# A new order of the attention stages of pairs 4 to 15, in a linear-attention and mixture-of-experts kernel

## The chip, the cores and the metric

The kernel runs on one core of a Trainium2 chip. A core has five engines with a queue each: TensorE (PE in the profile; PEld is its weight load), VectorE (DVE), ScalarE (ACT), GpSimd (POOL) and SyncE (SP), which here issues nearly all transfers. Each engine takes its instructions in the order of the program and stops at one whose inputs or buffers are not ready. The metric is the device time of one execution in microseconds.

## The reference

Two layers follow each other, in float32. The first is linear attention with batch 4, 8 heads, 576 tokens and head dimension 64; the second a mixture of 4 experts on the 2304 tokens.

```
phi(x):  p = x @ w_phi;  p = p - max|p| over the 128 features
         return concat(exp(p), exp(-p))                # 256 features
q_p, k_p = phi(q), phi(k)
kv  = sum over tokens of k_p^T v        z = sum over tokens of k_p
num = q_p @ kv      den = q_p . z + 1e-6      attn = num / den
x = attn as [2304, 512];  p = domain_probs / (row sum + 1e-9)
out = sum over e of  p[:, e] * (relu(x @ w1[e]) @ w2[e])     # 512 -> 1024 -> 512
```

## The kernel before

**Work.** Attention goes by pairs: one pair is two heads of one batch entry, 16 in all (four batch entries of four pairs). The second layer goes by units: a unit is two blocks of 128 hidden features of one expert, 16 units for each block of tokens. `first_units` runs all 16 units on the first 512 tokens while the attention of pairs 5 to 15 still runs; `second_units` then takes the other tokens in a form with fewer products (seven instead of eight, with sums of blocks, `x_ops` and `s_sums`).

**Float32 out of rounded parts.** Most matmuls take a number as a rounded part (hi) and a rest (lo), and form three products. So each operand needs a rounding copy (`split_pair`, `exps`, `w_hi`) and a subtraction (`lo_part`, `w_lo`).

**The stages of a pair.** `load_pair` fetches keys, queries and values. `split_pair` makes hi and lo. Keys: `proj` (three groups of token tiles), `proj_sub` (maximum and subtraction on VectorE, which frees the bank), `k_exp` on ScalarE, `k_kv` on TensorE; `kv_hi` and `kv_lo` split the result. Queries of pairs 4 to 15 are stacked: hi and lo of one head lie in the two halves of the partitions, so `q_proj` gets the transposed projection at once. There the maximum runs across partitions: `q_max` copies the projection to `dq` on ScalarE and reduces on VectorE, `q_maxT` transposes the partial maxima on TensorE, `q_maxrow` reduces again and writes them to memory (`max_d`), `q_maxin` reads them back into all partitions (`mb`), `q_sub` subtracts them, `q_exp2` takes both exponentials and rounds, `lo_part` makes the rest. Then `q_num` (score products), `q_copy`, and for the denominators a way through memory: `den_out`, `den_in`, `den_recip`, `rec_out`, `rec_in`; `x_mul` is the product of the two, `x_out` and `x_store` pass it on. The queries and the scores have three parts: (0, 0) for the first 256 tokens of both heads, (1, 0) and (1, 1) for the other 320 of each.

**What sets the order.** The schedule is written by hand. Each stage has a key, an offset within the pair plus 16 for each pair, and `later` puts it into a heap. The units give the pace: after each step of three 512-wide matmuls `tick` moves the clock by `clock.step` keys and `run_until` emits all stages whose key has come. So the keys fix the order of each engine's queue, not times. `LAST` (the last `x_out`) sets `clock.step`; after `LAST_IN` (the last use of the attention's input buffers) `to_early` reuses their space, loads tokens for the second stage, and its sums `xa_ops` follow at one key each; `to_late` does the same for the rest.

**Buffers that matter here.** Three PSUM banks `ps_att` serve ten users in a pair of the stacked kind: three key projections, three query projections, the transposed maxima, three score products. The second layer's matmuls (`l2_tile`, L668) have two banks, freed by `out` on VectorE (L678). The exponentials have two buffers `e` (freed by `lo_part`, L330) and five buffers `ehi`, which the keys' exponentials share. Low parts run on VectorE for part (0, 0) and on GpSimd for the two others (`LO_ENG`).

Of the kernel before, what the change touches and what calls it, by code (L numbers as in the profile page):

```python
# [20 lines left out]
def kernel(  # L21
# [16 lines left out]
    nc = tc.nc  # L38
# [9 lines left out]
    NPAIR = B * NP  # L48
# [5 lines left out]
    PER = 16  # L54
# [36 lines left out]
    max_d = dram.tile([NPAIR, 2 * S], F32, name="max_d")  # L91
# [13 lines left out]
    def later(key, fn):  # L105
        heapq.heappush(queue, (key, next(count), fn))

    def run_until(key):
        while queue and queue[0][0] <= key:
            heapq.heappop(queue)[2]()  # L110
# [22 lines left out]
    pairs = [Pair() for _ in range(NPAIR)]  # L133
# [113 lines left out]
    def q_maxrow(i):  # L247
        s = pairs[i]
        s.mrow = ap_.tile([S // 16, 32], F32, name="mrow", tag="mrow", bufs=1)
        nc.vector.tensor_reduce(  # L250
            s.mrow, s.mT[0 : S // 16, 0:P].rearrange("p (a c) -> p c a", c=32), axis=AX.X, op=ALU.max
        )
        nc.sync.dma_start(max_d[i].rearrange("(r c) -> r c", c=32), s.mrow)

    def q_maxin(i):
        s = pairs[i]
# [68 lines left out]
    def lo_part(i, parts, op):  # L325
        engine = {"v": nc.vector, "g": nc.gpsimd}[(LO_ENG0 if i < NP else LO_ENG)[op]]
        if len(parts) > 1:
            e, sl = parts[1]
            lo = ap_.tile([P, 1024], F32R, name="elo", tag="elo", bufs=4)
            engine.tensor_tensor(lo[sl], e[sl], parts[0][sl].bitcast(F32), op=ALU.subtract)  # L330
            parts[1] = lo

    def k_exp(i, c):
        s = pairs[i]
        t4, t4z = (slice(0, 64), slice(64, P)) if s.stack else (slice(64, P), slice(0, 64))
        rows, g = (slice(0, P), 4) if c < 2 else (t4, 2)
        d = s.d["k", c][rows, : g * NF]
        s.ke[c] = exps(d.rearrange("p (g f) -> p g f", f=NF), rows, g, NF, False)
        if c == 2:

            nc.gpsimd.memset(s.ke[c][0][t4z, : 2 * g * NF], 0.0)
# [159 lines left out]
    def x_store(i):  # L501
# [4 lines left out]
        if a < t0 + S:  # L506
            nc.sync.dma_start(xd[hp, :, a : t0 + S], pairs[i].xt[:, a - t0 :])

    STAGES = (
        (-25.6, load_pair, ("kq",)),  # L510
        (-16, load_pair, ("v",)),
        (-7.5, split_pair, ("k",)),
        (-1.9, split_pair, ("q",)),
        (-0.3, proj, ("k", 0)), (0.6, proj_sub, ("k", 0)), (2.7, k_exp, (0,)),
        (7.2, k_kv, (0,)),
        (2.1, proj, ("k", 1)), (2.1, proj_sub, ("k", 1)), (3.9, k_exp, (1,)),
        (10, k_kv, (1,)),
        (2.8, proj, ("k", 2)), (3.4, proj_sub, ("k", 2)), (8.3, k_exp, (2,)),
        (12.2, k_kv, (2,)), (13, kv_hi, ()), (13.2, kv_lo, ()),
    )  # L520
    TAIL = (
        (18.6, q_num, (0, 0)), (19.9, q_copy, (0, 0)),
        (21.5, q_num, (1, 0)), (22, q_copy, (1, 0)),
        (22.7, q_num, (1, 1)), (23.3, q_copy, (1, 1)),
        (26.2, den_out, ()), (29.8, den_in, ()), (31.2, den_recip, ()), (32.5, rec_out, ()),
        (34.7, rec_in, ()), (36.9, x_mul, ()), (40.5, x_store, ()), (37, x_out, ()),
    )
    Q_STAGES = (
        (5.5, proj, ("q", 0)), (6.4, proj_sub, ("q", 0)), (8.4, q_tr, (0, 0)), (9.4, q_exp, (0, 0)),
        (13.7, lambda i: lo_part(i, pairs[i].qe[0, 0], 0), ()),  # L530
        (7.5, proj, ("q", 1)), (10.4, proj_sub, ("q", 1)),
        (14.5, q_tr, (1, 0)), (15.2, q_exp, (1, 0)),
        (16, lambda i: lo_part(i, pairs[i].qe[1, 0], 1), ()),
        (14.5, q_tr, (1, 1)), (15.5, q_exp, (1, 1)),
        (16, lambda i: lo_part(i, pairs[i].qe[1, 1], 2), ()),
    )
    STACK_STAGES = (
        (4.4, q_proj, (0, 0)), (5.2, q_max, (0, 0)),
        (5, q_proj, (1, 0)), (5.8, q_max, (1, 0)),
        (6.6, q_proj, (1, 1)), (7.3, q_max, (1, 1)),  # L540
        (8.6, q_maxT, ()), (9, q_maxrow, ()), (10, q_maxin, ()),
        (13.5, q_sub, (0, 0)), (13.7, q_exp2, (0, 0)),
        (13.9, q_sub, (1, 0)), (14.3, q_exp2, (1, 0)),
        (14.7, lambda i: lo_part(i, pairs[i].qe[0, 0], 0), ()),
        (14.5, q_sub, (1, 1)), (15, q_exp2, (1, 1)),
        (15.4, lambda i: lo_part(i, pairs[i].qe[1, 0], 1), ()),
        (15.8, lambda i: lo_part(i, pairs[i].qe[1, 1], 2), ()),
    )
    SHIFT = 3.5
    for i in range(NPAIR):  # L550
        stack = pairs[i].stack
        for o, fn, args in STAGES + (STACK_STAGES if stack else Q_STAGES):
            later(PER * i + o, functools.partial(fn, i, *args))
        for o, fn, args in TAIL:
            later(PER * i + o + (SHIFT if stack else 0), functools.partial(fn, i, *args))
    FIRST = PER * (NP - 1) + 37
    LAST = PER * (NPAIR - 1) + 37 + SHIFT
    LAST_PS = PER * (NPAIR - 1) + 24 + SHIFT
    LAST_IN = PER * (NPAIR - 1) + 16.1

# [80 lines left out]
    def convert(kind, n, wait):  # L644
# [3 lines left out]
        if kind == "w1" and n >= NU:  # L648
            for o, fn in ((wait[0], s_sums), (wait[0] + 0.5, s_hi), (wait[1], s_lo)):
                later(max(clock.key, LAST + XA_LATE + 1) + o * clock.step, functools.partial(fn, n))  # L650
        else:
# [3 lines left out]
    def l2_tile(n, h, j, tile, o):  # L655

        e = (n % NU) * 2 // NFC
        if n >= NU and tile % 3 == 0:
            ps = ps_kv.tile([P, DM], F32, name="l2", tag="kv")
        elif n < NU and clock.key > LAST_PS:  # L660

# [136 lines left out]
    def spread(ops, start, gap):  # L798
        for i, fn in enumerate(ops):
            after(start + gap * i, fn)  # L800
# [132 lines left out]
    with tc.manual_schedule():  # L933
        nc.vector.memset(wbd, 0.0)
        nc.sync.dma_start(wbd[0:D, 0:NF], w_phi)
        nc.scalar.dma_start(wbd[D:P, NF : 2 * NF], w_phi)
        nc.vector.memset(out0[:, 0, 0:256], 0.0)
        warm = ps_l2.tile([P, 512], F32, name="warm", tag="l2")
        for _ in range(4):
            nc.tensor.matmul(  # L940
                warm[:, 0:256], lhsT=out0[:, 0, 0:P], rhs=out0[:, 0, 0:256], start=True, stop=True
            )
        run_until(STAGES[0][0])
        make_identity(nc, ident)
        nc.vector.memset(eps, 0.0)
        nc.vector.memset(eps[64:P, 0:1], 1e-6)
        nc.vector.memset(eps[0:64, 1:2], 1e-6)
        nc.vector.tensor_copy(wbd_hi, wbd)
        nc.vector.tensor_tensor(wbd_lo, wbd, wbd_hi.bitcast(F32), op=ALU.subtract)
        later(2.1, lambda: nc.sync.dma_start(pr, probs.rearrange("(t p) e -> p t e", p=P)))  # L950

        def probs_norm():
            nc.vector.reduce_sum(prs, pr, axis=AX.X)
            nc.vector.tensor_scalar_add(prs, prs, 1e-9)
            nc.vector.reciprocal(prs, prs)
            nc.vector.tensor_tensor(
                pr, pr, prs.unsqueeze(2).to_broadcast([P, NTT, NE]), op=ALU.mult
            )

        later(20.1, probs_norm)  # L960
        later(30.1, stacked_weights)
        for n in range(2):
            for i, kind in enumerate(("w1", "w2")):
                for o, fn in ((0, w_load), (4, w_hi), (6, w_lo)):
                    later(FETCH[2 * n + i] + o, functools.partial(fn, kind, n))
        run_until(FIRST)
        xa, xb = Pair(), Pair()
        xa.first, xa.nt = N0, 512
        xb.first, xb.nt = N0 + 8, 384
        for x, hi, lo in ((xa, x1_hi, x1_lo), (xb, x0_hi, x0_lo)):  # L970
            x.op = {
                "B11": (hi[:, 0:2, : x.nt], lo[:, 0:2, : x.nt]),
                "B21": (hi[:, 2:4, : x.nt], lo[:, 2:4, : x.nt]),
            }
        out1 = []

        xa_ops = {}

        def to_early():

            in_stack.close()
            early.append(
                ctx.enter_context(
                    tc.tile_pool(name="early", bufs=1, side="right", reuse_waits="tile")
                )
            )
            x_load(xa, xa.first + 4, xa.nt)
            xa_ops.update(x_ops(xa))
            fns = [fn for k in ("t", "T2", "T1", "t3", "T3") for fn in xa_ops[k]]
            for i, fn in enumerate(fns):  # L990
                later(LAST_IN + X_IN + X_GAP * i, fn)

        def to_late():

            att_stack.close()
            late.append(ctx.enter_context(tc.tile_pool(name="late", bufs=1, reuse_waits="tile")))
            out1.append(late[0].tile([P, 4, DM], F32, name="out1"))

        later(LAST_IN, to_early)
        later(LAST + XA_LATE, to_late)  # L1000
        clock.key = FIRST
        clock.step = (LAST - FIRST) / (NU * (2 * NP + 2 * N0) * SPREAD)
        pend = first_units()
        clock.key = max(clock.key, LAST + XA_LATE)
        run_until(clock.key)
        clock.step = 1
        spread([fn for k in ("B22", "t4", "T4") for fn in xa_ops[k]], XA_START, XA_GAP)
        second_units(pend)
# [38 lines left out]
```

## Time and profile before

| | |
|---|---|
| median of 3 runs | 1042.74 us (1041.63 to 1043.3) |
| profiled execution | 1037.1 us |
| its span | 1035.3 us |
| mean granted TensorE clock | 0.967 |
| busy: TensorE, VectorE, ScalarE, GpSimd | 971.7, 667.2, 456.7, 529.9 us |

In 40 equal slices of the span, in tenths, TensorE's busy share, VectorE's, ScalarE's and the granted clock are:

```profile
PE   9987778999889889989999999999989999999998
DVE  6455455556555657786776666667886776766764
ACT  5555554455555554343433333333343443443441
PEclk9897899999999999999999999999999999999999
```

A slice is 25.9 us. The first 15 or so are attention with the first units, the rest is the second stage. An idle time in the trace stands in brackets before the instruction that ended it, with the engine and line that released it.

### The profile page before, as it was taken

Reading aid. Unit: us, or ns where it says so; the run is one execution under the profiler, and the core shown is the slowest. Engines: PE = TensorE matmul, PEld = TensorE weight load, DVE = VectorE, ACT = ScalarE, POOL = GpSimd, SP = SyncE. Lnnn points to the kernel's source line nnn. Section 1 sums busy time; section 2 is a strip of 40 time slices with the busy share of each in tenths; the row PEclk is TensorE's granted clock in tenths of the full one; section 3 lists DMA queues with packets and bytes.
Section 4 is the critical chain, followed back from the end, with each engine's and each line's share of the span. In section 5 each row is a group of like instructions: output and inputs, shape, how many; then the busy total and the mean of one; then the engine's idle time right before and its main releaser. Section 6 shows DMA issues by size and latency. Waiting matters only on the chain. (4 is left out here: it accounts for less than half of the span.)

```text
span 1035.3 us, 13384 instructions
## 1 busy us (share of the span) xinstructions
PE 971.7 (94%) x4883; PEld 836.3 (81%) x4883; DVE 667.2 (64%) x1027; ACT 456.7 (44%) x832; POOL 529.9 (51%) x391
## 2 busy tenths in 40 slices
PE   9987778999889889989999999999989999999998
PEld 7887667788777778768888888888878888888887
DVE  6455455556555657786776666667886776766764
ACT  5555554455555554343433333333343443443441
POOL 3543454364455444665455445544474656556551
PEclk9897899999999999999999999999999999999999
DMA  6443235444444325333112111211114122112111
GB/s 152 131 114 113 79 85 146 126 125 135 129 109 132 103 71 178 88 106 101 49 41 92 61 41 49 65 51 41 55 51 139 62 62 82 62 61 80 59 45 61
DMA packets 74641, 91.42 MB, mean 88 GB/s; under 512 B 35120, under 2 KB 37040, under 8 KB 74576
## 3 DMA queue, kind: packets, MB, share of 16 engines
q1 hardware_dynamic: 74496, 90.55, 29.5%
q8 instruction: 38, 0.62, 0.3%
q14 instruction: 27, 0.22, 0.1%
q10 hardware_dynamic: 80, 0.03, 0.0%
HBM read 83.01 MB, written 7.54 MB: 87 GB/s over the span
## 5 line engine op out<-in xcount | busy, mean ns | idle before, releaser
L678 DVE SCALAR_TENSOR_TENSOR out<-l,pr,out 128x512 f32<-128x512 f32 x270 | 199.5, 746 | 107.9 <-PE l L668 107.2
L668 PE MATMUL l<-w2hi,h_lo 128*128 128x512 f32 x576 | 230.7, 401 | 21.0 <-DVE out L678 20.8
L668 PE MATMUL l<-w2hi,h_hi 128*128 128x512 f32 x576 | 229.8, 399 | 0.0
L668 PE MATMUL l<-w2lo,h_hi 128*128 128x512 f32 x576 | 229.1, 398 | 0.1
L668 PEld LDWEIGHTS l<-w2hi,h_lo 128*128 128x128 f32 x576 | 110.6, 192 | 42.5 <-DVE out L678 24.7
L668 PEld LDWEIGHTS l<-w2hi,h_hi 128*128 128x128 f32 x576 | 110.1, 191 | 23.8
L631 POOL TENSOR_TENSOR w1lo<-wraw,w1hi 128x512 fp32r<-128x512 f32 x64 | 77.1, 1224 | 96.1 <-ACT w1hi L623 58.3
L668 PEld LDWEIGHTS l<-w2lo,h_hi 128*128 128x128 f32 x576 | 110.7, 192 | 18.3 <-POOL w2lo L594 0.6
L594 POOL TENSOR_TENSOR w2lo<-wraw,w2hi 128x1024 fp32r<-128x1024 f32 x48 | 115.5, 2407 | 11.3 <-ACT w2hi L588 6.3
L826 ACT ACTIVATE h_hi<-c 128x512 fp32r<-128x512 f32 (+1 forms) x96 | 55.0, 578 | 68.8 <-DVE c L823 67.8
L353 PEld LDWEIGHTS kv<-v,e 128*128 128x128 f32 x640 | 81.3, 199 | 3.2
L836 POOL TENSOR_TENSOR c<-u,s 128x512 f32<-128x512 f32 (+1 forms) x32 | 37.2, 1162 | 84.8 <-DVE u L823 84.8
L353 PE MATMUL kv<-v,e 128*128 128x66 f32 x640 | 79.8, 279 | 0.0
L631 POOL TENSOR_TENSOR s_lo<-ws,s_hi 128x768 fp32r<-128x768 f32 x32 | 58.9, 1841 | 30.7 <-ACT s_hi L623 30.7
L196 POOL TENSOR_TENSOR qs<-qr,qs 64x1152 fp32r<-64x1152 f32 x12 | 32.0, 2671 | 82.9 <-issue 53.8
L852 ACT ACTIVATE c<-c 128x512 f32<-128x512 f32 (+1 forms) x32 | 18.5, 580 | 126.0 <-POOL c L836 126.0
L691 DVE SCALAR_TENSOR_TENSOR h_lo<-l,h_hi 128x512 fp32r<-128x512 f32 x32 | 21.9, 688 | 79.3 <-ACT h_hi L721 79.3
L833 POOL TENSOR_TENSOR h_lo<-c,h_hi 128x512 fp32r<-128x512 f32 (+1 forms) x32 | 37.5, 1173 | 40.2 <-ACT h_hi L826 40.2
L691 DVE SCALAR_TENSOR_TENSOR h_lo<-c,h_hi 128x512 fp32r<-128x512 f32 (+1 forms) x64 | 56.2, 878 | 2.2 <-ACT h_hi L826 2.1
L318 ACT ACTIVATE e<-d 128x512 f32<-128x512 f32 (+1 forms) x96 | 47.7, 549 | 15.1 <-DVE d L301 14.9
L588 ACT ACTIVATE w2hi<-wraw 128x1024 fp32r<-128x1024 f32 x48 | 50.5, 1052 | 8.4 <-PE l L668 8.3
L704 PE MATMUL l<-x_hi,w1lo 128*128 128x512 f32 x128 | 52.3, 409 | 0.0
(161 smaller groups left out, 2214.8 us busy)
## 6 DMA issues: line engine op xcount, KB each, us to landing
wraw<-in_w_dram SPq DMA_DIRECT2D x96, 512.0 KB
mb<-max_d SPq DMA_DIRECT2D x12, 576.0 KB
qr<-in_kq_dram SPq DMA_DIRECT2D x24, 256.0 KB
rb<-rec_d SPq DMA_DIRECT2D x32, 144.0 KB
out_dram<-out SPq DMA_DIRECT2D x18, 256.0 KB
v<-in_v_dram SPq DMA_DIRECT2D x32, 128.0 KB
kr<-in_kq_dram SPq DMA_DIRECT2D x12, 320.0 KB
xd<-rb SPq DMA_DIRECT2D x8, 288.0 KB
```

What stands on the lines that cost most here:

```text
L318: nc.scalar.activation(to, src, AF.Exp, scale=1.0 - 2 * sg)
L353: nc.tensor.matmul(s.kv[:, n * KW : (n + 1) * KW], lhsT=e[:, e0 : e0 + NF], rhs=s.v[:, t, h * KW : (h + 1) * KW], start=(c == 0 and j == 0 ...
L588: nc.scalar.activation(hi, raw, AF.Copy)
L594: nc.gpsimd.tensor_tensor(lo, raw, hi.bitcast(F32), op=ALU.subtract)
L631: nc.gpsimd.tensor_tensor(dst, src, hi.bitcast(F32), op=ALU.subtract)
L668: nc.tensor.matmul(ps, lhsT=l[:, f, j * P : (j + 1) * P], rhs=r[:, f, :], start=(f == 0 and k == 0), stop=(f == 1 and k == 2),)
L678: nc.vector.scalar_tensor_tensor(o, ps, p, o, op0=ALU.mult, op1=ALU.add)
L691: nc.vector.scalar_tensor_tensor(lo, src, 0.0, hi.bitcast(F32), op0=ALU.max, op1=ALU.subtract)
L704: nc.tensor.matmul(banks[n, f], lhsT=l[:, ksl], rhs=r[:, k, :], start=(k == 0 and j == 0), stop=(k == NP - 1 and j == 2),)
L826: nc.scalar.activation(h[b][0][:, f, :nt], src, AF.Relu)
L833: nc.gpsimd.tensor_tensor(dst, src, hi.bitcast(F32), op=ALU.subtract)
L836: nc.gpsimd.tensor_tensor(temp("c22"), c["u3"], c["s5"], op=ALU.add)
```

## The change

The stages of pairs 0 to 3 go into a list `OLD`, with four keys altered. Those of pairs 4 to 15 get a list of their own, `NEW`, with new keys throughout. The write of the row maximum becomes a stage `q_maxout`, apart from `q_maxrow`, and the low parts a stage `q_lo`. `SHIFT` (3.5 keys on the last stages of the stacked pairs) is gone, and the old keys named below include it. `LAST`, `LAST_PS` and `LAST_IN` follow from the list: `LAST` goes from 280.5 to 279.37, `LAST_IN` from 256.1 to 262.95. No operation, engine or buffer count is changed.

```diff
-        nc.sync.dma_start(max_d[i].rearrange("(r c) -> r c", c=32), s.mrow)
+
+    def q_maxout(i):
+        nc.sync.dma_start(max_d[i].rearrange("(r c) -> r c", c=32), pairs[i].mrow)
...
+    def q_lo(i, part, h):
+        lo_part(i, pairs[i].qe[part, h], part + h)
...
-    STAGES = (
-        (-25.6, load_pair, ("kq",)),
-        (-16, load_pair, ("v",)),
-        (-7.5, split_pair, ("k",)),
-        (-1.9, split_pair, ("q",)),
...
-    TAIL = (
-        (18.6, q_num, (0, 0)), (19.9, q_copy, (0, 0)),
-        (21.5, q_num, (1, 0)), (22, q_copy, (1, 0)),
-        (22.7, q_num, (1, 1)), (23.3, q_copy, (1, 1)),
-        (26.2, den_out, ()), (29.8, den_in, ()), (31.2, den_recip, ()), (32.5, rec_out, ()),
-        (34.7, rec_in, ()), (36.9, x_mul, ()), (40.5, x_store, ()), (37, x_out, ()),
-    )
...
-    STACK_STAGES = (
-        (4.4, q_proj, (0, 0)), (5.2, q_max, (0, 0)),
-        (5, q_proj, (1, 0)), (5.8, q_max, (1, 0)),
-        (6.6, q_proj, (1, 1)), (7.3, q_max, (1, 1)),
-        (8.6, q_maxT, ()), (9, q_maxrow, ()), (10, q_maxin, ()),
-        (13.5, q_sub, (0, 0)), (13.7, q_exp2, (0, 0)),
-        (13.9, q_sub, (1, 0)), (14.3, q_exp2, (1, 0)),
-        (14.7, lambda i: lo_part(i, pairs[i].qe[0, 0], 0), ()),
-        (14.5, q_sub, (1, 1)), (15, q_exp2, (1, 1)),
-        (15.4, lambda i: lo_part(i, pairs[i].qe[1, 0], 1), ()),
-        (15.8, lambda i: lo_part(i, pairs[i].qe[1, 1], 2), ()),
-    )
-    SHIFT = 3.5
+    NEW = (
+        (-22.75, load_pair, ("kq",)),
+        (-15.3, load_pair, ("v",)),
+        (-10.5, split_pair, ("k",)),
+        (-5.8, split_pair, ("q",)),
+        (-0.7, proj, ("k", 0)), (-0.6, proj_sub, ("k", 0)), (2.7, k_exp, (0,)),
+        (6.94, k_kv, (0,)),
+        (0.52, proj, ("k", 1)), (2.55, proj_sub, ("k", 1)), (4.04, k_exp, (1,)),
+        (11.24, k_kv, (1,)),
+        (2.8, proj, ("k", 2)), (4.64, proj_sub, ("k", 2)), (8.74, k_exp, (2,)),
+        (12.48, k_kv, (2,)), (12.48, kv_hi, ()), (14.03, kv_lo, ()),
+        (2.01, q_proj, (0, 0)), (6.04, q_max, (0, 0)),
+        (6.24, q_proj, (1, 0)), (6.24, q_max, (1, 0)),
+        (7.19, q_proj, (1, 1)), (7.19, q_max, (1, 1)),
+        (9.04, q_maxT, ()), (9.04, q_maxrow, ()), (9.89, q_maxout, ()), (10.44, q_maxin, ()),
+        (11.88, q_sub, (0, 0)), (14.38, q_exp2, (0, 0)),
+        (13.23, q_sub, (1, 0)), (16.63, q_exp2, (1, 0)),
+        (16.45, q_lo, (0, 0)),
+        (13.43, q_sub, (1, 1)), (19.9, q_exp2, (1, 1)),
+        (17, q_lo, (1, 0)),
+        (22.85, q_lo, (1, 1)),
+        (24.95, q_num, (0, 0)), (26.65, q_copy, (0, 0)),
+        (26.15, q_num, (1, 0)), (26.9, q_copy, (1, 0)),
+        (26.24, q_num, (1, 1)), (26.94, q_copy, (1, 1)),
+        (30.24, den_out, ()), (31.27, den_in, ()), (32.22, den_recip, ()), (35.58, rec_out, ()),
+        (36.98, rec_in, ()), (37.55, x_mul, ()), (44.4, x_store, ()), (39.37, x_out, ()),
+    )
```

In `OLD` the split of the queries goes from -1.9 to -5, and three keys move by 0.05. A key above 16 belongs, in the order of the queues, to the next pair: the score products at 24.95 stand where the next pair is at 8.95.

## Rows read from the trace of the kernel before

**Rows 1.** The page, part 1: busy us, share of the span and instructions.

```profile
PE 971.7 (94%) x4883; PEld 836.3 (81%) x4883; DVE 667.2 (64%) x1027; ACT 456.7 (44%) x832; POOL 529.9 (51%) x391
```

**Rows 2.** Busy time by stretch: start:end, us, then each engine, clock, DMA share, GB/s.

```profile
98.60:387.30 288.70, 251.56 (x1436) 218.51 (x1436) 158.28 (x279) 156.41 (x282) 141.09 (x95) 0.94 0.41 115
...
176.00:192.00 16.00, 11.49 (x62) 10.14 (x63) 11.94 (x17) 9.26 (x17) 9.87 (x7) 0.89 0.26 79
...
320.00:336.00 16.00, 14.52 (x93) 12.43 (x91) 9.62 (x18) 7.65 (x16) 9.22 (x8) 1.00 0.47 124
```

**Rows 3.** TensorE's timeline, idle times: start, us, instruction, [idle before, releaser].

```profile
115.21 0.71 PE L222 MATMUL projT<-qs,wst 128*128 128x256 f32 x4 [2.27 <-DVE d L301]
121.76 0.87 PE L222 MATMUL projT<-qs,wst 128*128 128x320 f32 x2 [5.03 <-DVE rec L465]
...
180.51 0.50 PE L668 MATMUL l<-w2hi,h_lo 128*128 128x512 f32 x1 [4.56 <-DVE out L678]
...
322.20 0.53 PE L222 MATMUL projT<-qs,wst 128*128 128x320 f32 x2 [1.37 <-DVE rec L465]
347.20 0.50 PE L668 MATMUL l<-w2hi,h_lo 128*128 128x512 f32 x1 [3.03 <-DVE out L678]
```

**Rows 4.** VectorE's timeline before the gap that ends at 180.5.

```profile
171.18 0.68 DVE L264 TENSOR_TENSOR dq<-dq,mb 128x512 f32<-128x512 f32 x1
...
176.15 3.65 DVE L330 TENSOR_TENSOR elo<-e,ehi 128x1024 fp32r<-128x1024 f32 x1
179.72 0.74 DVE L678 SCALAR_TENSOR_TENSOR out<-l,pr,out 128x512 f32<-128x512 f32 x1
```

**Rows 5.** ScalarE's and GpSimd's timelines before the gap that ends at 121.8.

```profile
117.48 0.83 ACT L318 ACTIVATE e<-dq 128x320 f32<-128x320 f32 x2 [5.67 <-POOL elo L330]
...
112.73 3.22 POOL L594 TENSOR_TENSOR w1lo<-wraw,w1hi 128x1024 fp32r<-128x1024 f32 x1
115.92 1.53 POOL L330 TENSOR_TENSOR elo<-e,ehi 128x640 fp32r<-128x640 f32 x1
```

**Rows 6.** TensorE's timeline, starts at full clock.

```profile
164.57 1.89 PE L353 MATMUL kv<-v,e 128*128 128x66 f32 x16
166.27 0.40 PE L435 MATMUL num<-ehi,kvlo 128*128 128x320 f32 x1
...
167.23 0.40 PE L704 MATMUL l<-x_hi,w1lo 128*128 128x512 f32 x1
167.47 0.40 PE L704 MATMUL l<-x_lo,w1hi 128*128 128x512 f32 x1
```

**Rows 7.** VectorE's timeline, row maximum and the subtraction that waits for it.

```profile
74.31 0.28 DVE L250 TENSOR_REDUCE mrow<-maxT 36x32 f32<-36x128 f32 x1
79.62 1.50 DVE L264 TENSOR_TENSOR dq<-dq,mb 128x512 f32<-128x512 f32 x3 [0.64 <-DMA mb<-max_d]
...
304.65 0.28 DVE L250 TENSOR_REDUCE mrow<-maxT 36x32 f32<-36x128 f32 x1
312.18 0.94 DVE L264 TENSOR_TENSOR dq<-dq,mb 128x512 f32<-128x512 f32 x1 [0.44 <-DMA mb<-max_d]
```

**Rows 8.** The low parts' line: durations ns min/median/max; GpSimd beside the 3.65 us one.

```profile
L330 DVE TENSOR_TENSOR elo<-e,ehi x12: 1224/1226/3647, 82.7 to 399.0; 128x1024 fp32r<-128x1024 f32 x12
...
175.89 2.82 POOL L196 TENSOR_TENSOR qs<-qr,qs 64x1152 fp32r<-64x1152 f32 x1 [6.77 <-issue]
```

**Rows 9.** SP's timeline, first and last of a pair's five key and query loads.

```profile
242.50 0.58 SPq L147 DMA_DIRECT2D kr<-in_kq_dram  x1
...
245.16 0.61 SPq L154 DMA_DIRECT2D qr<-in_kq_dram  x1
```

**Rows 10.** Reciprocal and product of pair 15 on VectorE; busy time by stretch there.

```profile
420.82 0.20 DVE L465 RECIPROCAL rec<-den 128x9 f32<-128x9 f32 x1
...
427.62 2.52 DVE L484 TENSOR_TENSOR rb<-nd,rb 64x576 f32<-64x576 f32 x2 [2.92 <-DMA rb<-rec_d]
...
400.00:410.00 10.00, 10.00 (x55) 8.76 (x54) 9.97 (x13) 4.88 (x10) 6.36 (x3) 1.00 0.28 85
```

More of the change, by code (lines that the diff above doesn't have):

```diff
@@ L507, in x_store @@
             nc.sync.dma_start(xd[hp, :, a : t0 + S], pairs[i].xt[:, a - t0 :])
-    STAGES = (
+    OLD = (
         (-25.6, load_pair, ("kq",)),
@@ L512 @@
         (-7.5, split_pair, ("k",)),
-        (-1.9, split_pair, ("q",)),
+        (-5, split_pair, ("q",)),
         (-0.3, proj, ("k", 0)), (0.6, proj_sub, ("k", 0)), (2.7, k_exp, (0,)),
         (7.2, k_kv, (0,)),
-        (2.1, proj, ("k", 1)), (2.1, proj_sub, ("k", 1)), (3.9, k_exp, (1,)),
+        (2.1, proj, ("k", 1)), (2.15, proj_sub, ("k", 1)), (3.9, k_exp, (1,)),
         (10, k_kv, (1,)),
@@ L519 @@
         (12.2, k_kv, (2,)), (13, kv_hi, ()), (13.2, kv_lo, ()),
-    )
-    TAIL = (
+        (5.5, proj, ("q", 0)), (6.4, proj_sub, ("q", 0)), (8.4, q_tr, (0, 0)), (9.4, q_exp, (0, 0)),
+        (13.7, q_lo, (0, 0)),
+        (7.5, proj, ("q", 1)), (10.4, proj_sub, ("q", 1)),
+        (14.5, q_tr, (1, 0)), (15.2, q_exp, (1, 0)),
+        (16, q_lo, (1, 0)),
+        (14.55, q_tr, (1, 1)), (15.5, q_exp, (1, 1)),
+        (16.05, q_lo, (1, 1)),
         (18.6, q_num, (0, 0)), (19.9, q_copy, (0, 0)),
@@ L527 @@
     )
[L528 to L535, printed above, removed]
-    )
-    STACK_STAGES = (
-        (4.4, q_proj, (0, 0)), (5.2, q_max, (0, 0)),
-        (5, q_proj, (1, 0)), (5.8, q_max, (1, 0)),
-        (6.6, q_proj, (1, 1)), (7.3, q_max, (1, 1)),
-        (8.6, q_maxT, ()), (9, q_maxrow, ()), (10, q_maxin, ()),
-        (13.5, q_sub, (0, 0)), (13.7, q_exp2, (0, 0)),
-        (13.9, q_sub, (1, 0)), (14.3, q_exp2, (1, 0)),
-        (14.7, lambda i: lo_part(i, pairs[i].qe[0, 0], 0), ()),
-        (14.5, q_sub, (1, 1)), (15, q_exp2, (1, 1)),
-        (15.4, lambda i: lo_part(i, pairs[i].qe[1, 0], 1), ()),
-        (15.8, lambda i: lo_part(i, pairs[i].qe[1, 1], 2), ()),
-    )
@@ L550 @@
     for i in range(NPAIR):
-        stack = pairs[i].stack
-        for o, fn, args in STAGES + (STACK_STAGES if stack else Q_STAGES):
+        for o, fn, args in NEW if pairs[i].stack else OLD:
             later(PER * i + o, functools.partial(fn, i, *args))
-        for o, fn, args in TAIL:
-            later(PER * i + o + (SHIFT if stack else 0), functools.partial(fn, i, *args))
+    at = {(fn, args): o for o, fn, args in NEW}
     FIRST = PER * (NP - 1) + 37
-    LAST = PER * (NPAIR - 1) + 37 + SHIFT
@@ L558 @@
-    LAST_PS = PER * (NPAIR - 1) + 24 + SHIFT
-    LAST_IN = PER * (NPAIR - 1) + 16.1
+    LAST = PER * (NPAIR - 1) + at[x_out, ()]
+    LAST_PS = PER * (NPAIR - 1) + at[q_num, (1, 1)] + 1.3
+    LAST_IN = PER * (NPAIR - 1) + max(at[q_lo, (1, h)] for h in range(2)) + 0.1
     NU = NE * NFC // 2
@@ L942 @@
             )
-        run_until(STAGES[0][0])
+        run_until(OLD[0][0])
         make_identity(nc, ident)
```

## The prediction

> **What bounds the kernel now.** I read the busy table first: TensorE is busy for 94% of the span, VectorE for 64%, ScalarE for 44% [rows 1]. So no second engine is near a bound over the whole, and time can only come out of TensorE's idle time and its clock. The slices of the page show both losses in the first 40% of the span, where attention pairs and the first 16 units share the engines; from about 500 us on TensorE hardly waits.
>
> The second view is busy time by stretch, taken from the row-maximum of pair 5 (98.6 us) to that of pair 15 (387.3 us): ten whole pairs, 288.7 us, 28.9 us each [rows 2]. TensorE is busy for 251.6, so idle for 37.1. Its granted clock is 0.94. With two levels, 2.4 and 1.2 GHz, that is 12% of the stretch at the lower one, 34.6 us; at half speed and a busy share of 0.87 that loses 34.6 x 0.87 / 2 = 15 us. **The loss in the stretch is 52 us, 5.2 a pair; without it a pair would take 23.7 us.**
>
> The third view is TensorE's timeline with its idle times. There are 16 gaps: eight of 2.2 to 5.1 us, 29 us together, the first at 115.2 and the last at 347.2, and eight under 1.4 us, 7.7 together, of which the 1.37 at 322.2 is the largest [rows 3]. Four of the long ones end with VectorE's `out`, four with its key sums or the reciprocal among them. The clock goes with the long ones: the 16 us from 176, which hold a gap of 4.56, have 0.89, and the 16 us that hold the 1.37 gap have 1.00 [rows 2, 3]. Eight long gaps cost 15 us of clock, 1.9 each.
>
> The fourth view is what the releasing engine did in such a gap. At 180.5 TensorE waits for a bank of the second layer. VectorE's `out`, which frees it, runs at 179.7, behind score subtractions and a low-part subtraction (`elo`) of 3.65 us; the first subtraction was at 171.2 [rows 4]. The cause is the order: three subtractions, three exponential groups and three low parts stand within 2.3 keys (13.5 to 15.8), so VectorE waits for ScalarE and ScalarE for VectorE, with the `out`s of the units behind them. At 121.8 it is the other face of this: ScalarE stood 5.67 us before the third exponential, since the two `e` buffers were held until GpSimd's low part (115.9) had run, itself behind a weight's low part of 3.22 us from 112.7 [rows 5]. VectorE's sums and bank releases wait behind ScalarE.
>
> **The change part by part.** No instruction is added or removed; a stage keeps its operations, and only places in the queues change. Sixteen keys are a pair. I go through TensorE's order with its spacing: a step of three 512-wide matmuls starts 0.24 apart, 0.7 us; 16 kv products take 1.70 us, one of the two later score products 0.96 [rows 6].
>
> *Exponentials spread out* (13.7, 14.3, 15 become 14.38, 16.63, 19.9; low parts 14.7, 15.4, 15.8 become 16.45, 17, 22.85). The third exponential now stands behind the first two low parts in the program, with about three keys between, so the buffer wait is gone in the order itself. VectorE's low part stands 4.6 keys after its subtraction (1.2 before), so ScalarE's two exponentials and rounding are done when VectorE comes to it. The key sums of the next pair now stand ahead of it. I laid out two pairs by hand, one with the second layer across the row maximum and one with it just before. In the first, with t = 0 where its key projection starts, TensorE without a wait is at the first score product at 12.4 and at the maximum's transpose at 13.8. VectorE's queue to there is the first key sum (0.8 to 2.1), the low part (to 3.4, or 5.8 if stretched), two `out`s and two key sums (to 7.5), the next pair's rounding and the product (to 9.5), one `h_lo` and the first maximum (to 10.9, or 12.7), the last one at 12.2 or 13.7: banks are free in time, with 0.1 us to spare or 0.3 short at the worst. The second pair is alike. These are estimates from the durations of this trace (0.7 an `out` or a `h_lo`, 1.3 a key sum, 1.5 the product). **The long gaps end with exactly the two things that stood behind this knot, `out`s and key sums; I take all eight out: 29 + 15 = 44 us.** The bound on the other side is 0, if each gives way to an equal wait.
>
> *Stacked queries sooner* (split at 10.2 instead of 14.1, first projection at 2.01 instead of 4.4). GpSimd's part has 7.8 keys until its use, as before, but stands ahead of the low parts instead of among them. The projection holds one of three attention banks from 2.01 until its maximum at 6.04, four keys instead of 0.8. With two banks left the other projections still find the one freed by a sum two stages earlier; I cost it at 0 and keep 1.4 us a pair as the worst, the size of the small gaps.
>
> *Small gaps.* I leave the eight under 1.4 us as they are, 0 gained of 7.7.
>
> *The maximum's round trip.* The row-maximum goes to memory and comes back for the subtraction. That took 5.03 us (74.59 to 79.62) and 7.25 (304.93 to 312.18) where VectorE waited for it [rows 7]. The distance falls from 4.5 keys to 2.84, and VectorE blocks there. TensorE has 3.3 steps, two score products and 16 kv products between: 2.3 + 1.9 + 1.7 = 5.9 us, and 2.2 more until it needs an `out` that is queued behind: 8.1. VectorE needs 5.0 to 7.25 plus the maximum, the subtraction, a kv copy and the `out`, 0.3 + 0.6 + 0.4 + 0.7: 7.0 to 9.3. So -1.1 to +1.2 us, and only for pairs with the second layer there, about half: **cost 3 us of 0 to 6.**
>
> *The low part beside GpSimd.* Eleven of VectorE's 12 ran in about 1.23 us; the one beside GpSimd's query split took 3.65 [rows 4, 8]. In the old order the others waited for ScalarE while GpSimd stood still. Now GpSimd's own low part and weights fall beside it. Up to 2.4 us a pair, 24 in all; VectorE's slack in my two pairs takes most of it: **cost 4 us of 0 to 24.**
>
> *Three score products together* (22.1, 25, 26.2 become 24.95, 26.15, 26.24). They take all banks that the maxima free; their inputs are ready 2 keys ahead, copies follow on ScalarE. 0, with the same 1.4 us a pair as worst case.
>
> *Loads, denominators.* Loads leave SP when the entry before allows, not at their key; the five of a pair take 3.3 us of issuing (242.5 to 245.8 [rows 9]) and lead by over 12 keys: 0. Reciprocal to product was 6.8 us with the wait seen (420.8 to 427.6 [rows 10]); 5.3 keys are 7.9 us at 23.7 a pair: 0, worst case in the second rival.
>
> *The end of attention.* The last input key moves from 256.1 to 262.95, so the combinations for the second stage start 6.85 keys later while the first units end where they did. VectorE is at 9.97 of 10 us there [rows 10]. A step is 0.863 keys now (0.868 before), so 6.85 keys are 8 steps or 5.6 us of TensorE; where VectorE sets the end, each us that it starts later comes out there. 0 if its wait of 2.92 us [rows 10] and other slack swallow it; 10 if the shorter way from the last score products to the reciprocal (5.3 keys, 7.9 before) adds a wait as long as that one and more: **6 us lost, of 0 to 10.** For pair 4, where no unit fills in yet, a longer wait for the maximum and the earlier query cancel: 0.
>
> **Sum:** 44 - 3 - 4 - 6 = 31 us. The profiled execution took 1037.1 us, 1.8 around a span of 1035.3; so 1006 there. The median of the runs is 5.6 above the profiled one, which I add: **1011.5 us.**
>
> **Rivals.** *The shared port rules (1031 us).* For: the 3.65 row, and that GpSimd is busy half of the time. Against: 11 of 12. If every low part stretches and nothing absorbs it, 24 is lost instead of 4: gain 11. The Trainium skill (GPSIMD Engine Reference, Specifications) says that GpSimd shares its SBUF interfaces with VectorE and contends with VectorE instructions that read two SBUF inputs. By that rule this rival is the forecast, since the low part is of that kind; the one row beside GpSimd agrees, the eleven others were not beside it.
>
> *VectorE's loop of two round trips (1061 us, slower).* In each pair VectorE's queue goes maximum, trip, subtraction, reciprocal, trip, product, next maximum. VectorE works 15.8 us a pair [rows 2]; of that I count 7.5 inside the trips, by the places of its stages (an estimate): 8.3 + 7.25 + 6.8 = 22.4 us, just under 23.7. If SP puts the five loads (3.3 us; key 9.25, directly ahead of the maximum's write at 9.89) and the four v loads (2.6 by the same spacing) in front of the two writes, it is 28.3, and TensorE's gap of over 4 us in each pair brings its clock loss, 1.9: 30.2 against 28.9, ten pairs 13 us, the end 6: 1042.7 + 19, near 1061. It decides when a gap is above some 3 us in every pair. Against it: SP runs ahead and should have issued the loads before the maximum is there.
>
> *The wait only moves (1040 us).* Banks held for four keys or the bunched products give a pair a new wait of about 4 us with its clock loss. For: three banks for ten users a pair. Against: every release stands two stages ahead in the program.
>
> **How the numbers follow.** Forecast 0.62, its own range 995 to 1027 (low end: nothing of the 13 us of costs, and some small gaps too). Port 0.15, moved wait 0.11, loop 0.12. From 992 to 1041 leaves out the loop, a little of the moved wait and a low tail, 0.2. I call 0.2% what a measurement can tell: faster is the forecast, the port and half of the moved wait, 0.82; same 0.05; slower 0.13.
>
> **What would show it.** After: the stretch between the maxima of pairs 5 and 15 near 250 us with clock 0.98 or more; no wait of ScalarE's `e` on a low part; `out` no longer the longest releaser of TensorE; VectorE's wait on `mb`, 0.64 and 0.44 us where shown [rows 7], one or two us in most pairs. The low parts' mean on VectorE tells the port. The forecast is wrong if TensorE's idle time in the stretch stays above 25 us, or if the end, from the last score product to the second units, grows by more than 10.

## The result and the profile after

The changed kernel takes 992.44 us (median of 4 runs, 984.22 to 995.28) against 1042.18 us: ratio 0.9512, interval 0.9453 to 0.957. In a second set of runs it was 986.8 us against 1037.21, ratio 0.9515 (0.9483 to 0.9547). The forecast was 1011.5 us, so its sign was right and its gain, 31 us, too small: about 50 were gained. The profiled execution took 991.64 us, with a span of 989.9.

The page of the changed kernel, part 1, answers to [rows 1]: TensorE's share goes from 94 to 97%, and its busy time falls by 16 us though it executes the same instructions.

```profile
PE 955.9 (97%) x4883; PEld 824.9 (83%) x4883; DVE 683.8 (69%) x1027; ACT 455.5 (46%) x832; POOL 542.1 (55%) x391
```

Busy time by stretch, first the changed kernel, then two stretches of the kernel before that [rows 2] left out. The cuts are the row maxima of pairs 5 and 15 and a point in the second stage.

```profile
0.00:94.30 94.30, 82.00 (x503) 74.29 (x504) 50.59 (x96) 56.68 (x117) 44.91 (x55) 0.91 0.51 135
94.30:342.50 248.20, 239.64 (x1439) 210.81 (x1439) 182.31 (x277) 153.20 (x280) 148.10 (x94) 0.99 0.48 133
342.50:420.00 77.50, 70.80 (x327) 58.09 (x325) 61.92 (x77) 35.07 (x60) 43.44 (x28) 0.98 0.36 116
420.00:989.90 569.90, 563.41 (x2616) 481.72 (x2616) 388.94 (x577) 210.60 (x376) 305.67 (x216) 1.00 0.20 64
```

```profile
0.00:98.60 98.60, 85.45 (x509) 78.04 (x510) 55.60 (x98) 56.04 (x117) 43.00 (x53) 0.86 0.47 124
387.30:465.00 77.70, 71.16 (x325) 57.86 (x323) 61.38 (x76) 33.31 (x58) 43.43 (x28) 0.98 0.40 122
```

The ten pairs between the maxima take 248.2 us instead of 288.7, 40.5 less. TensorE is idle for 8.6 us there (37.1 before), which is 28.6 of it; its busy time is 239.6 instead of 251.6 for the same work, which goes with the clock, 0.99 instead of 0.94, and makes the other 11.9. The part ahead is 4.3 us shorter, the rest after pair 15's maximum 0.6 (647.4 after 648.0). The sum, 45.4, is the difference of the two spans.

TensorE's largest waits in the stretch before, and all of them after (instruction, releaser: us in total, times, longest):

```profile
PE l L668 <- DVE out L678: 16.9, 5, 5.1
PE projT L222 <- DVE rec L465: 8.7, 3, 5.0
PE projT L222 <- DVE d L301: 6.4, 3, 3.3
...
```

```profile
PE num L440 <- DVE bm L237: 5.5, 6, 2.3
PE l L680 <- DVE out L690: 2.0, 2, 1.3
PE projT L222 <- DVE d L303: 1.0, 1, 1.0
```

The second layer's wait for `out` fell from 16.9 to 2.0 us. What is left is new: the first score product waits for the bank that a query maximum frees. VectorE in turn now waits for the maximum's way through memory; before there were three such waits, 1.3 us in all (two of them in [rows 7]), and after the change the largest of ten (28.0 us in total) is this one:

```profile
318.60 0.28 DVE L250 TENSOR_REDUCE mrow<-maxT 36x32 f32<-36x128 f32 x1 [0.36 <-PE maxT L245]
...
325.08 0.69 DVE L266 TENSOR_TENSOR dq<-dq,mb 128x512 f32<-128x512 f32 x1 [5.81 <-DMA mb<-max_d]
```

### The profile page after: what moved, and what is told of

Read it like the earlier page. It is cut to its first block, busy times and chain, and to the rows that moved or that the text cites. A ratio compares the mean times of both kernels' runs of the same rounds, so it can differ in the third digit from the quotient of the medians.

```text
span 989.9 us, 13384 instructions
## 1 busy us (share of the span) xinstructions
PE 955.9 (97%) x4883; PEld 824.9 (83%) x4883; DVE 683.8 (69%) x1027; ACT 455.5 (46%) x832; POOL 542.1 (55%) x391
## 5 line engine op out<-in xcount | busy, mean ns | idle before, releaser
L680 PE MATMUL l<-w2hi,h_lo 128*128 128x512 f32 x576 | 226.8, 394 | 3.9 <-DVE out L690 3.8
L680 PE MATMUL l<-w2hi,h_hi 128*128 128x512 f32 x576 | 226.3, 393 | 0.0
L680 PE MATMUL l<-w2lo,h_hi 128*128 128x512 f32 x576 | 226.1, 392 | 0.0
L643 POOL TENSOR_TENSOR w1lo<-wraw,w1hi 128x512 fp32r<-128x512 f32 x64 | 79.8, 1267 | 92.9 <-ACT w1hi L635 55.1
L680 PEld LDWEIGHTS l<-w2lo,h_hi 128*128 128x128 f32 x576 | 108.6, 188 | 17.5
L332 POOL TENSOR_TENSOR elo<-e,ehi 128x640 fp32r<-128x640 f32 x24 | 42.7, 1780 | 49.5 <-ACT ehi L324 45.0
L635 ACT ACTIVATE s_hi<-ws 128x768 fp32r<-128x768 f32 x32 | 27.1, 848 | 62.6 <-DVE ws L619 62.6
L606 POOL TENSOR_TENSOR w1lo<-wraw,w1hi 128x1024 fp32r<-128x1024 f32 x16 | 40.1, 2506 | 25.1 <-ACT w1hi L600 25.0
L886 PE MATMUL A<-x_hi,w1lo 128*128 128x512 f32 (+1 forms) x128 | 47.7, 373 | 6.2 <-ACT s L832 3.7
```

The costliest lines, as they stand in the source:

```text
L606: nc.gpsimd.tensor_tensor(lo, raw, hi.bitcast(F32), op=ALU.subtract)
L643: nc.gpsimd.tensor_tensor(dst, src, hi.bitcast(F32), op=ALU.subtract)
L680: nc.tensor.matmul(ps, lhsT=l[:, f, j * P : (j + 1) * P], rhs=r[:, f, :], start=(f == 0 and k == 0), stop=(f == 1 and k == 2),)
L886: nc.tensor.matmul(ps, lhsT=l[:, k * P : (k + 1) * P], rhs=r[:, k, :], start=(k == 0 and j == 0 and not again), stop=(k == 1 and j == 2), ...
```

## The experiments

Each was timed beside the kernel before. "Stretch" is the time from pair 5's maximum to pair 15's in its profiled execution: 288.7 us before, 248.2 and (second set) 246.3 with the whole change. So two executions of one program can differ by 2 us in it.

**Exponentials alone.** The prediction put the whole gain on the knot of subtractions, exponentials and low parts. So: the kernel before with these moved, and nothing else but the last input key.

```diff
-        (13.5, q_sub, (0, 0)), (13.7, q_exp2, (0, 0)),
...
+        (11.88, q_sub, (0, 0)), (14.38, q_exp2, (0, 0)),
+        (13.23, q_sub, (1, 0)), (16.63, q_exp2, (1, 0)),
...
+        (13.43, q_sub, (1, 1)), (19.9, q_exp2, (1, 1)),
...
-    LAST_IN = PER * (NPAIR - 1) + 16.1
+    LAST_IN = PER * (NPAIR - 1) + 22.95
```

> The kernel before with only the subtractions, exponentials and low parts of pairs 4 to 15 at their new keys (and the last input key that follows from them). Theory A, the knot of these stages makes the long gaps: most of the gain comes with this move alone, ratio to before 0.955 to 0.97, stretch between the maxima of pairs 5 and 15 at 250 to 262 us. Rival B, the gain needs the earlier queries and the regrouped scores too: ratio 0.98 to 1.0, stretch above 275 us.

Measured: 1020.53 us, ratio 0.9844 (0.9801 to 0.9887), stretch 271.3. Theory A missed. The ratio lies in the rival's range, the stretch in neither: 17.4 of 40.5 us. The stretch and TensorE's largest waits in it:

```profile
98.55:369.85 271.30, 246.33 (x1437) 212.39 (x1436) 174.82 (x278) 155.46 (x282) 144.88 (x95) 0.97 0.42 122
...
PE l L668 <- DVE out L678: 8.0, 5, 3.6
PE projT L222 <- DVE d L301: 5.8, 5, 3.0
PE projT L222 <- POOL elo L330: 4.6, 2, 3.1
PE projT L222 <- DVE bm L237: 3.0, 4, 1.1
...
```

The 5 us waits are gone, but TensorE stops at others: at the query projections, for banks. That holds for the two put down to GpSimd's `elo`, too. A query projection does not read `elo`; the query split that it does read had ended 5.55 and 3.56 us before, while VectorE's key sum, which frees a bank, ended some 0.15 us before each projection began.

**Exponentials back.** The opposite: the whole change without this move.

```diff
-        (11.88, q_sub, (0, 0)), (14.38, q_exp2, (0, 0)),
-        (13.23, q_sub, (1, 0)), (16.63, q_exp2, (1, 0)),
-        (16.45, q_lo, (0, 0)),
...
+        (13.5, q_sub, (0, 0)), (13.7, q_exp2, (0, 0)),
+        (13.9, q_sub, (1, 0)), (14.3, q_exp2, (1, 0)),
+        (14.7, q_lo, (0, 0)),
...
```

> The changed kernel with subtractions, exponentials and low parts of pairs 4 to 15 at their old keys, the last input key held at the new one. Theory A: the long gaps come back, 25 us or more of idle TensorE in the stretch, ratio to before 0.98 to 1.0. Rival B (the other moves carry the gain): ratio 0.95 to 0.97.

Measured: 1015.0 us, ratio 0.9796 (0.9756 to 0.9836), stretch 270.3, idle 24.2. Both lie just under theory A's marks (0.98 and 25 us), and far from rival B's. Without the move 22 us of the gain are lost; the 18 that stay are what theory A does not explain.

**The last input key.** The kernel before with only that line changed.

```diff
-    LAST_IN = PER * (NPAIR - 1) + 16.1
+    LAST_IN = PER * (NPAIR - 1) + 22.95
```

> The kernel before with only the last input key moved from 256.1 to 262.95, as the changed kernel has it. As the prediction had it: 6 us slower (ratio 1.006), because VectorE is full where the sums for the second stage go later. Rival: VectorE has room, ratio 0.998 to 1.002.

Measured: 1038.97 us, ratio 1.002 (0.9987 to 1.0052); after pair 15's maximum 647.6 us (648.0 before). The rival holds as far as the profile tells: there is no 6 us, though the interval of the ratio does not exclude a few.

**Queries late again.** The whole change, with split, projections and maxima of the queries at their old keys.

```diff
-        (-5.8, split_pair, ("q",)),
+        (-1.9, split_pair, ("q",)),
...
-        (2.01, q_proj, (0, 0)), (6.04, q_max, (0, 0)),
+        (4.4, q_proj, (0, 0)), (5.2, q_max, (0, 0)),
...
```

> The changed kernel with the query split at -1.9 and query projections and maxima at their old keys (4.4 to 7.3). Theory A: the earlier queries matter little, ratio to before 0.95 to 0.96. Rival: GpSimd's query split behind the low parts makes TensorE wait as before (some 2 us a pair), ratio 0.97 to 0.98.

Measured: 999.14 us, ratio 0.9642 (0.9595 to 0.969), stretch 257.3: 9 us of the stretch come back, between the two expectations. The waits are not at GpSimd, as the rival had it, but at VectorE:

```profile
PE l L680 <- DVE out L690: 8.3, 6, 2.9
PE maxT L245 <- DVE bm L237: 6.3, 6, 1.8
PE projT L222 <- DVE d L303: 1.7, 2, 1.4
```

**Exponentials and queries together, on the kernel before.**

```diff
-        (4.4, q_proj, (0, 0)), (5.2, q_max, (0, 0)),
+        (2.01, q_proj, (0, 0)), (6.04, q_max, (0, 0)),
...
-        (8.6, q_maxT, ()), (9, q_maxrow, ()), (10, q_maxin, ()),
+        (9.04, q_maxT, ()), (9.04, q_maxrow, ()), (10.44, q_maxin, ()),
```

> The kernel before with two of the moves: exponentials spread, and queries split, projected and reduced at the new keys. Theory C (after the first four runs): each move takes waits of its own, so the two add: exponentials alone left the stretch at 271.3 us, taking the queries back cost the changed kernel 9.1, so 260 to 265 us here, ratio to before 0.972 to 0.98. Rival: the early queries help only together with the key stages; stretch 268 to 272, ratio 0.983 or more.

Measured: 1015.83 us, ratio 0.9803 (0.9762 to 0.9845), stretch 267.6: the ratio is at the edge of theory C's range, the stretch just under the rival's. Beside exponentials alone the queries give 3.7 us here; inside the whole change they were worth 9. In place of the old waits the next pair's key projections wait for banks:

```profile
PE proj L287 <- DVE d L301: 11.8, 7, 2.8
PE l L669 <- DVE out L679: 7.8, 3, 4.5
```

**Key stages back.** The whole change with the keys' split, projections, sums, exponentials and products at their old places.

```diff
-        (-0.7, proj, ("k", 0)), (-0.6, proj_sub, ("k", 0)), (2.7, k_exp, (0,)),
+        (-0.3, proj, ("k", 0)), (0.6, proj_sub, ("k", 0)), (2.7, k_exp, (0,)),
...
```

> The changed kernel with the key stages of pairs 4 to 15 (key split, projections, sums, exponentials, products) at their old keys. Theory C with the 14 us that neither exponentials nor queries explain lying here (the first key sum ahead of VectorE's low part): stretch 256 to 262 us against 248.2, ratio 0.96 to 0.97. Rival: they lie with the score products; stretch under 252, ratio as the changed kernel.

Measured: 992.64 us, ratio 0.9578 (0.9524 to 0.9633), stretch 253.7: some 5 us, mostly at `out` (7.7 us in 5 waits; 2.0 with the whole change). That is less than theory C had it and more than the rival.

**Score products apart.** The whole change with the three score products and copies at their old keys.

```diff
-        (24.95, q_num, (0, 0)), (26.65, q_copy, (0, 0)),
-        (26.15, q_num, (1, 0)), (26.9, q_copy, (1, 0)),
-        (26.24, q_num, (1, 1)), (26.94, q_copy, (1, 1)),
+        (22.1, q_num, (0, 0)), (23.4, q_copy, (0, 0)),
+        (25, q_num, (1, 0)), (25.5, q_copy, (1, 0)),
+        (26.2, q_num, (1, 1)), (26.8, q_copy, (1, 1)),
```

> The changed kernel with score products and their copies at their old keys (22.1, 25, 26.2). Theory C with the rest in the key stages: stretch 247 to 252 us, ratio as the changed kernel; the waits of the first score product for a maximum's bank (5.5 us) go or move. Rival, the products together carry the rest: stretch 256 to 262, ratio 0.96 to 0.97.

Measured: 1002.76 us, ratio 0.9677 (0.9634 to 0.9721), stretch 259.9. The rival holds: 12 us lie in where the score products stand. The query projections now wait for the bank that an earlier maximum frees:

```profile
PE projT L222 <- DVE bm L237: 10.9, 9, 2.4
PE l L680 <- DVE out L690: 2.8, 3, 2.2
PE num L440 <- DVE d L303: 1.8, 2, 1.0
```

**Only the first score product early.** To see which of the three does it.

```diff
-        (24.95, q_num, (0, 0)), (26.65, q_copy, (0, 0)),
+        (22.1, q_num, (0, 0)), (23.4, q_copy, (0, 0)),
```

> The changed kernel with only the first score product and its copy at their old keys (22.1, 23.4), so that it stands between the first and the second query projection; the two later products stay together. Theory D, a score product there takes one of the three banks out of the projections' turn: nearly all of what taking all three apart cost (11.7 us) comes back, stretch 256 to 261, with TensorE's projections waiting for maxima. Rival: the bunching of the two later products matters; stretch under 252.

Measured: 996.41 us, ratio 0.9588 (0.9541 to 0.9636), stretch 254.0, between the two expectations. That is 6 to 8 us of the 12, and the largest wait is the same one:

```profile
PE projT L222 <- DVE bm L237: 8.9, 8, 2.1
...
```

With key 22.1 the product stands at 6.1 of the next pair, before the second query projection at 6.24. It takes a bank out of the three while the first projection still holds one until its maximum at 6.04. So theory D has the mechanism, and somewhat more than half of the size; the rest should belong to the two later products, which were not moved by themselves.

**Subtractions back.** The whole change with the three subtractions at their old keys, so that VectorE has other work while the maximum travels.

```diff
-        (11.88, q_sub, (0, 0)), (14.38, q_exp2, (0, 0)),
-        (13.23, q_sub, (1, 0)), (16.63, q_exp2, (1, 0)),
+        (13.5, q_sub, (0, 0)), (14.38, q_exp2, (0, 0)),
+        (13.9, q_sub, (1, 0)), (16.63, q_exp2, (1, 0)),
...
-        (13.43, q_sub, (1, 1)), (19.9, q_exp2, (1, 1)),
+        (14.5, q_sub, (1, 1)), (19.9, q_exp2, (1, 1)),
```

> The changed kernel with only the three subtractions at their old keys (13.5, 13.9, 14.5). VectorE then has more to do before it waits for the maximum's round trip (28 us of such waits in the changed kernel). As the prediction had it, that wait costs TensorE 3 us: stretch 243 to 247. Rival: VectorE's wait lies in its slack, and later subtractions push ScalarE's exponentials together: stretch 250 to 256.

Measured: 991.25 us, ratio 0.9555 (0.9517 to 0.9592), stretch 244.9. VectorE's line for this wait went from ten times to one:

```profile
  DMA mb<-max_d: 0.9, 1
```

The stretch was inside the first expectation, but the whole change was not repeated in that set. So both ran once more, with more rounds.

> The changed kernel once more, to set the two others of this call beside it: ratio to before 0.945 to 0.96. Also its stretch between the maxima, 247 to 250 us, and the time before the first of them, which moved between 91 and 97 us in kernels that share that part.

> The changed kernel with the subtractions at their old keys, once more and with more rounds: theory, VectorE's wait for the maximum costs TensorE some 3 us, so 0.3% under the changed kernel of this call. Rival: no difference, within 0.1%.

Measured: the whole change 986.8 us, ratio 0.9515 (0.9483 to 0.9547), stretch 246.3; with the subtractions back 986.65 us, ratio 0.952 (0.9479 to 0.9562), stretch 245.9. TensorE is idle for 7.2 and 6.4 us of the two stretches. There is no difference that these runs can tell, though the intervals do not exclude 3 us: some 27 us of waiting on VectorE cost TensorE nothing measurable.

**The first maximum ahead of the product.** On top of that, an attempt at the last wait.

```diff
-        (2.01, q_proj, (0, 0)), (6.04, q_max, (0, 0)),
+        (2.01, q_proj, (0, 0)), (5.52, q_max, (0, 0)),
```

> The same with the first query maximum at 5.52 instead of 6.04, ahead of the product with the reciprocals on VectorE. If the first score product's remaining waits (3.2 us in six) come from a maximum that stands behind that product, they go: stretch 241 to 244. Rival: ScalarE's copy sets the maximum anyway, and the stretch stays at 244 to 247.

Measured: 1000.48 us, ratio 0.9652 (0.9616 to 0.9687), stretch 258.8: both expectations missed. Half a key cost 13 us of the stretch against the run without it (245.9). The first score product's wait is gone from the list, and longer ones have come, above all that of the transposed maxima for the last maximum:

```profile
PE maxT L245 <- DVE bm L237: 10.6, 8, 2.2
PE l L680 <- DVE out L690: 6.1, 2, 4.9
PE projT L222 <- DVE d L303: 0.4, 1, 0.4
```

The last maximum stood behind the product on VectorE before, too. What is new is that the product takes longer: 33.9 us for the ten of the stretch, against 27.8. In one pair, without the move and with it:

```profile
232.97 2.80 DVE L489 TENSOR_TENSOR rb<-nd,rb 64x576 f32<-64x576 f32 x2
...
241.92 3.81 DVE L489 TENSOR_TENSOR rb<-nd,rb 64x576 f32<-64x576 f32 x2
```

Of the two halves of that product, one began while GpSimd was computing in the first case, and both in the second (see the last section).

## Why the prediction was right in sign and too small

The miss of 19 us has four parts, by the profiled executions: 3.5 in the stretch (37 us forecast, 40.5 measured), 6.6 after pair 15's maximum (6 lost forecast, 0.6 gained), 4.3 ahead of pair 5's maximum (0 forecast), and 4.8 from the step between profile and median: I added the 5.6 us that lay between them before, and after the change there were 0.8. That last part is chance (which execution was profiled), and most of the 4.3 may be.

So the steps that failed in the sum are these. The end, put at 6 us lost, cost nothing. The small gaps, put at 0 gained of 7.7, went with the long ones: of the waits before, only 2.0 us for `out` and 1.0 for a key sum have a counterpart after. The clock gave 11.9 us of the 15. The costs of the round trip and of GpSimd, put at 7, compare with the 8.6 us for which TensorE is still idle. That the 37 us forecast for the stretch came so near to 40.5 is in part luck, since these misses balance. In the mechanism, the step that failed is that the exponentials' move takes out all long gaps by itself.

**The loss to be had: right.** 52 us of idle and clock in the stretch, 5.2 a pair. 8.6 us of idle are left and the clock is 0.99; 24.8 us a pair stand against 23.7 without any wait. The expected marks, about 250 us and a clock of 0.98 or more, were met, and the clock came back with the long gaps, as the comparison of [rows 2] and [rows 3] had it.

**What takes it out: wrong in its attribution.** The step was that the knot of exponentials stood behind all long gaps and that its move alone removes them. It gives 17.4 us alone. Taken back from the whole, the moves cost 22 (exponentials), 12 (score products together), 9 (queries) and 5 us (key stages) of the stretch: 48, more than the 40.5 they give together (56 against the second profile of the whole change, which gives 42.4). The new keys of the loads and of the denominators' way were not tried by themselves. These are no independent costs: while one wait stands, it gives the others time, and when it goes, the next in the pair is what TensorE reaches. I had followed the releaser named at the gap, and not what would be late next. What the prediction said of the knot itself came: VectorE's waits for `ehi` at the low part, 12.0 us in the stretch before, are gone, and of ScalarE's waits for `elo`, one of 5.67 us before, three are left with 1.0 us at most.

**Score products and queries at 0: wrong.** I costed both as neutral, with 1.4 us a pair as the worst. The products are worth 12 us, by the turn of three banks among ten users. The same argument, a bank held longer, was in my list of rivals as a danger of the new order. It is a cost of the old product keys among the new query keys, where a product stands between two projections (10.9 us of waits); in the kernel before, that wait was 0.2 us. The earlier queries are worth 9 us. I took the way from their split to their projection as 7.8 keys "as before"; before, it was 6.3.

**The maximum's round trip at 3 us: too high, or at its low end.** The wait itself came, in ten of twelve pairs, with 2.8 us a time where one or two were expected. But it lies in VectorE's slack: without it, there is no difference in time (0.9515 and 0.952). The 2.0 us that TensorE still waits for `out` do not belong here: they are 2.0 with the subtractions back, too.

**The low part beside GpSimd at 4 us: not far off, but in another instruction.** The changed kernel's low parts, durations in ns (minimum, median, maximum), answer to [rows 8]:

```profile
L332 DVE TENSOR_TENSOR elo<-e,ehi x12: 1161/1192/3243, 81.4 to 352.6; 128x1024 fp32r<-128x1024 f32 x12
```

Four were stretched, to 1.84, 2.21, 2.48 and 3.24 us, some 5 us together, and eight were not. With the subtractions back (second run) that sum was some 2 us, and the time was the same. But VectorE's busy time in the stretch rose from 158.3 to 182.3 us for the same work, 24 us, which is the amount that the port rival had named for the low parts. Of VectorE's instructions two kinds took most of it: the product of `x_mul` (14.9 us for ten pairs before, 30.6 after) and the score subtractions (16.8 and 24.3). The product's line between 90 and 390 us, before and after (count, busy us, mean ns):

```profile
L484 DVE TENSOR_TENSOR rb<-nd,rb 64x576 f32<-64x576 f32 x22 | 17.6, 798 | 1.3 <-DMA rb<-rec_d 0.9
...
L489 DVE TENSOR_TENSOR rb<-nd,rb 64x576 f32<-64x576 f32 x24 | 34.6, 1443 | 3.0 <-DMA rb<-rec_d 2.6
```

The old keys put the key split, with its subtraction on GpSimd, just behind that product (8.5 and 8.4); the new ones put it just ahead (5.5 and 5.55), and the two run side by side. The prediction costed the product at 1.5 us. TensorE's longest wait after the change stands behind this one:

```profile
286.12 3.40 DVE L489 TENSOR_TENSOR rb<-nd,rb 64x576 f32<-64x576 f32 x2 [0.93 <-DMA rb<-rec_d]
...
290.98 0.39 PE L440 MATMUL num<-ehi,kvlo 128*128 128x256 f32 x1 [2.29 <-DVE bm L237]
```

All six waits of the first score product for a maximum's bank, 5.5 us, stand behind a stretched product, and all but this one are shorter than the time by which the product was stretched. So most of them may be the price of the contention; that is an estimate, since no run moved only the key split or the product. VectorE's slack took the rest of the 24 us, and with that the rival's time of 1031 us fell. The Trainium skill (GPSIMD Engine Reference, Specifications) has VectorE instructions with two SBUF inputs contend with GpSimd. The trace agrees that they do, and shows that who comes first decides who pays (last section).

**The end at 6 us lost: wrong, shown by its own experiment.** With only the last input key moved, the time after pair 15's maximum was 647.6 us against 648.0. VectorE is busy for 61.9 of 77.5 us in the whole stretch after the change and 61.4 of 77.7 before. I took 10 us in which it was full for the state of the whole end.

**The part ahead at 0: not settled.** It was 98.6 us before and 94.3 after, but 95.8 in the run with only the last input key moved, which shares all of that part with the kernel before, and 91.3 to 96.5 in the variants of the changed kernel. Some 3 us of the 4.3 can be the difference between executions. The changed keys of pairs 0 to 3 were not tried by themselves.

**The rivals.** VectorE's loop of two round trips did not close: its waits for both trips were there, and the one for the maximum cost TensorE nothing measurable. Those for the reciprocals (1.8 us in two, in the stretch) stand ahead of TensorE's two longest waits, 2.29 and 1.50 us, and may be part of them. The moved wait (1040 us) is what the partial kernels show, if less dearly: each has a new one. The whole order has one too, the first score product's, but of 5.5 us where TensorE's waits before were 36.8 in all.

## What to carry to other kernels

When several engines take turns on in-order queues and few buffers, a gap names the last link, not the cause. One move alone gave 17 us, a second on top of it 4, the whole 40; so cost a reorder as a whole, pair by pair, and ask of each wait that goes what is reached next. Look at who holds a bank in the order of its users as closely as at who computes: one product placed between two projections was worth 6 to 8 us, and half a key of a maximum cost 13. Look also at what another engine runs beside an instruction at its new place: the new keys made VectorE 24 us busier with the same work. An engine's waiting time (28 us here) says nothing until the bound engine waits behind it.

## What the runs showed of the hardware

A subtraction on VectorE and one on GpSimd, both from two SBUF inputs, do not share the time: the later one runs when the earlier is done. From the timelines of the changed kernel, GpSimd and VectorE at two places:

```profile
206.55 2.40 POOL L606 TENSOR_TENSOR w2lo<-wraw,w2hi 128x1024 fp32r<-128x1024 f32 x1
...
206.79 3.24 DVE L332 TENSOR_TENSOR elo<-e,ehi 128x1024 fp32r<-128x1024 f32 x1
...
230.57 2.03 POOL L332 TENSOR_TENSOR elo<-e,ehi 128x640 fp32r<-128x640 f32 x1 [4.46 <-DMA v<-in_v_dram]
...
230.01 1.16 DVE L332 TENSOR_TENSOR elo<-e,ehi 128x1024 fp32r<-128x1024 f32 x1
```

At 206.55 GpSimd starts first and ends at 208.95; VectorE's ends at 210.03, 1.08 us later, which is about what it takes alone. The three other stretched ones end 1.08 us after GpSimd's too, and so does the 3.65 us one of the kernel before (178.71 and 179.80, [rows 4, 8]). Of the other eleven there, one (at 112.45) had begun in the last 0.2 us of GpSimd's query split and took 1.29 us, so it was not quite apart from GpSimd, as the prediction had it. At 230.01 VectorE starts first and takes its 1.16 us, and GpSimd's takes 2.03 instead of about 1.58.

It is the same for VectorE's products and score subtractions. In the changed kernel 25 of these and of the low parts began at least 0.2 us before GpSimd's subtraction ended, and each ended 0.35 to 1.08 us after it, by its size, which is some 0.1 us less than it takes alone. VectorE's `out`, which reads a PSUM bank, does not wait: 168 of 270 began while GpSimd was computing, and these took 0.747 us on average, the others 0.746.
